# Hand-ordering an FFT-mixing and max-out-MLP kernel: an earlier first transform, a second buffer for its result, and a re-ordered startup

## The chip, the cores and the metric

The kernel runs on one core of one Trainium2 chip. The metric is device time in microseconds (us). Lower is better. The kernel before took 677.96 us (median of 15 runs). Runs of one kernel scatter: the kernel before stays within 674.8 to 683.2 us over 15 runs. So a single run says nothing about differences of a few us, and comparisons below use runs that were made on the same chip in turn. Experiments of different rounds are compared by their ratios to the kernel before, which ran in each round.

## The reference

For each of 8 batches, x (3072 x 256) is filtered along its length: real FFT, product with a filter, inverse FFT. The result goes through a two-branch max layer.

```python
X = np.fft.rfft(x, axis=1)                         # x: 8 x 3072 x 256
y = np.fft.irfft(X * (filt_r + 1j * filt_i), n=3072, axis=1)
x2 = y.reshape(8 * 3072, 256)
out = np.maximum(x2 @ w1, x2 @ w2) @ w_out         # w1, w2: 256 x 1024; w_out: 1024 x 256
```

## The kernel before

The length is split as 3072 = 128 x 24, so that the transforms become matmuls in four steps. Each batch passes through them like this:

- **f1** (12 pieces): `pa = C1 * x`, evicted (copied out of PSUM) by ScalarE (ACT) to `at`, written to DRAM as `ad`, and read back in another order as `bt`.
- **f2** (16 groups): `px = U * bt`; VectorE (DVE) multiplies by the filter `F` into `pqt`; `pz = VP * pqt + VQ * pqt` goes by way of `zt` to DRAM as `zd`, and is read back re-ordered as `zr`.
- **s4** (6 per batch): `py = zr * G1`, the last part of the inverse transform, giving `y` for one token tile.
- **moe** (6 tiles of 8 steps): `ph = Wd * y` with Wd = w1 - w2, a ReLU into `gt`, then `po = M * y + Wo * gt` with Wo = w_out and M = w2 * w_out, because max(a, b) = b + relu(a - b).

A batch of the main loop has 48 steps. In batch b the loop does moe for batch b, f2 for b+1 and f1 for b+2. A scheduler orders the instructions of each engine. PE is the matmul engine (TensorE). SP (SyncE) and POOL (GpSimd) mainly issue the DMA transfers here, each through its own queue, and POOL also makes tables.

```python
xpool = ...(name="xpool", bufs=2)     # x of one batch: 3 loads of 512 KB
apool = ...(name="apool", bufs=3)
bpool = ...(name="bpool", bufs=1)     # bt
...
def gen_f1(b):
    for c in range(12):
        ...                            # pa = C1 * x piece, at <- pa, every second c: ad <- at (SP)
        if c == 11:                    # then bt <- ad, 8 transfers on the SP queue
            ...
        yield
...
load_w(); load_x(1)
drain(gen_f1(0)); tables_pe(); prep_w()
...
drain(gen_f2(0)); drain(gen_f1(1)); s4(0)

for b in range(B + 1):
    ...
    for i in range(6):
        for j in range(8):
            moe_h(tt, j); moe_o(tt - 1, j)
            step = 8 * i + j
            if step % 2 == 0:
                next(f2, None)
            elif step >= 12:           # f1 of the batch after next starts here
                next(f1, None)
            if j == 4 and tt + 1 < 6 * B and i < 5:
                s4(tt + 1)
        if i == 5:
            drain(f2); drain(f1)
            s4(tt + 1)                 # first tile of the next batch, at the very end
```

## Time and profile before

| | before |
|---|---|
| span of the profiled run | 677.3 us |
| until the first px of the main loop | 134.3 us |
| from there to the end | 543.0 us |
| distance between first px of batches 0 and 1, 1 and 2 | 72.0, 72.4 us |

The first view is the page's row of 40 equal slices, here of 16.9 us each. A digit is the busy share in tenths. PEclk is the granted TensorE clock, and DMA is the mean busy share of the 16 DMA engines.

```profile
PE   0342293299987999699969996999989997999997
...
PEclk9856556589997999799979998899989998999999
DMA  9999528723495249623882369333842484234112
```

The left fifth is the startup: PE does little, and the DMA engines are at 9 in the first four slices. Later PE mostly reads 9, but falls to 6 or 7 again and again, and the clock falls with it. The chain of waits (what released what, followed back from the last instruction) sums to this, by engine:

```profile
PE 66%; DMA 22%; SPq 7%; ACT 2%; issue 1%; DVE 1%; DVEq 0%; ACTq 0%
```

22% of the span hangs on a DMA, though the matmuls are the work. The chain in order of time shows where. Its columns are the start in us, the length in us, and what. These are its longest pieces of the startup:

```profile
1.59 12.18 DMA w2f<-in_moe_w_dram
...
19.66 10.49 DMA ad<-at
...
50.94 9.19 SPq L273
60.17 9.87 SPq L273
...
74.41 5.78 DMA F<-zrow
...
108.32 11.04 DMA zr__600<-zd
119.44 4.29 DMA ad<-at
...
128.35 5.87 DMA bt__662<-ad
```

`SPq L273` is the SP queue issuing the `bt<-ad` transfers. Each of those two pieces takes over 9 us to issue. And these are successive pieces at the end of batch 1:

```profile
255.71 11.47 DMA zr__2076<-zd
267.25 4.10 DMA ad<-at
272.70 5.82 DMA bt__2125<-ad
278.65 0.63 PE px L298 x2
```

PE is not in this chain for about 23 us. For part of that it still has older work, but not to the end. The table of stretches shows this for the end of batch 0, where the chain leaves PE in the same way from 183.6 us on. Its columns are the stretch, its length, then busy us (and count) of PE, PE weight loads, DVE, ACT and POOL, the granted clock, the DMA share and GB/s:

```profile
200.00:206.50 6.50, 1.52 (x11) 0.87 (x9) 1.29 (x2) 0.00 (x0) 0.00 (x0) 0.87 0.86 190
206.50:214.00 7.50, 7.28 (x38) 4.75 (x39) 5.34 (x6) 3.35 (x6) 0.00 (x0) 0.66 0.42 80
```

PE works 1.5 of 6.5 us, and afterwards the granted clock averages 0.66 for 7.5 us. The start times of `px` by batch (minimum, median and maximum ns of one, then first and last start in us) give the period:

```profile
L298 PE MATMUL px<-bt__662,U x32: 270/274/417, 134.3 to 175.2; 96*96 96x256 bf16 x32
L298 PE MATMUL px<-bt__1305,U x32: 270/274/421, 206.3 to 247.2; 96*96 96x256 bf16 x32
L298 PE MATMUL px<-bt__2125,U x32: 270/274/421, 278.7 to 319.2; 96*96 96x256 bf16 x32
```

### The profile page before, as it was taken

The numbers are of one execution on the slowest core, as the hardware profiler recorded it, in microseconds if no ns is written. First come the engines' busy times: TensorE is split into PE (matmuls) and PEld (weight loads), VectorE is DVE, ScalarE is ACT, GpSimd is POOL, SyncE is SP. The second block draws the span as 40 slices with busy tenths as digits, with TensorE's granted clock in tenths as the row PEclk, the third lists the DMA queues.
The fourth block names the chain that finished last, engine by engine and source line by source line (L and its number), as shares of the span: only waits on it lengthen the run. The fifth ranks groups of instructions, "written<-read, shape, count | busy, mean of one in ns | idle before, by whom it ended". The sixth has DMA issues, their size and how long they took to land.

```text
span 677.3 us, 9992 instructions
## 1 busy us (share of the span) xinstructions
PE 548.2 (81%) x3939; PEld 402.7 (59%) x4008; DVE 362.0 (53%) x465; ACT 302.2 (45%) x537; POOL 30.3 (4%) x60
## 2 busy tenths in 40 slices
PE   0342293299987999699969996999989997999997
PEld 0131281177765777477647774677667775777775
DVE  2520280087636764477438742776377646864543
ACT  2450043156624663256416651566246634554441
POOL 5330000000000000000000000000000000000000
PEclk9856556589997999799979998899989998999999
DMA  9999528723495249623882369333842484234112
GB/s 233 135 135 193 112 70 193 184 54 143 128 252 120 99 144 227 172 86 112 206 210 101 126 160 235 89 115 139 199 110 98 145 203 116 68 129 124 63 63 93
DMA packets 82144, 94.51 MB, mean 140 GB/s; under 512 B 6737, under 2 KB 59986, under 8 KB 82002
## 3 DMA queue, kind: packets, MB, share of 16 engines
q1 hardware_dynamic: 73058, 77.62, 40.0%
q0 software_dynamic: 9040, 16.26, 16.8%
q8 instruction: 31, 0.51, 0.3%
q14 instruction: 15, 0.12, 0.1%
HBM read 59.77 MB, written 50.33 MB: 163 GB/s over the span
## 4 chain that ended last, share of the span: by engine, by line
PE 66%; DMA 22%; SPq 7%; ACT 2%; issue 1%; DVE 1%; DVEq 0%; ACTq 0%
PE ph L340 21%; PE po L365 19%; DMA ad<-at 6%; SPq L273 5%; PE px L298 5%; PE pz L288 5%; PE po L360 5%; PE pz L289 5%; PE py L324 3%; PE pa L264 2%; DMA w2f<-in_moe_w_dram 2%; DMA zr__2896<-zd 2%; DMA zr__1256<-zd 2%; DMA zr__2076<-zd 2%; DMA zr__600<-zd 2%
## 5 line engine op out<-in xcount | busy, mean ns | idle before, releaser
L365 PE MATMUL po<-Wo,gt 128*128 128x256 bf16 x1536 | 231.2, 273 | 1.1
L345 ACT ACTIVATE gt<-ph 128x512 bf16<-128x512 f32 x240 | 141.5, 593 | 161.2 <-PE ph L340 158.5
L301 DVE TENSOR_TENSOR pqt<-px,F 96x1024 bf16<-96x1024 f32 x128 | 155.5, 1218 | 96.6 <-PE px L298 75.5
L365 PEld LDWEIGHTS <-gt 128*128 128x128 bf16 x1536 | 149.8, 98 | 58.6 <-issue 1.4
L290 ACT ACTIVATE zt<-pz 96x512 bf16<-96x512 f32 x128 | 75.9, 593 | 132.3 <-PE pz L289 120.8
L343 DVE TENSOR_SCALAR gt<-ph 128x512 bf16<-128x512 f32 x144 | 99.0, 687 | 59.1 <-PE ph L340 55.3
L367 DVE COPY ot<-po 128x512 f32<-128x512 f32 x96 | 66.0, 691 | 89.4 <-PE po L365 69.2
L340 PEld LDWEIGHTS <-Wd 128*128 128x128 bf16 x768 | 76.0, 101 | 25.5 <-issue 6.6
L288 PE MATMUL pz<-pqt,VP 96*96 96x256 bf16 x256 | 70.7, 298 | 5.8 <-DVE pqt L301 5.6
L289 PE MATMUL pz<-pqt,VQ 96*96 96x256 bf16 x256 | 71.1, 300 | 0.0
L298 PEld LDWEIGHTS <-U 96*96 96x96 bf16 x256 | 34.3, 141 | 59.5 <-issue 42.0
L265 ACT ACTIVATE at<-pa 128x512 bf16<-128x512 f32 x96 | 55.5, 598 | 28.5 <-PE pa L264 13.3
L289 PEld LDWEIGHTS <-VQ 96*96 96x96 bf16 x256 | 34.7, 135 | 8.7 <-issue 7.4
L288 PEld LDWEIGHTS <-VP 96*96 96x96 bf16 x256 | 35.1, 137 | 1.4 <-DVE pqt L301 0.7
L264 PEld LDWEIGHTS <-C 128*128 128x128 bf16 x96 | 10.3, 108 | 23.8 <-ACT C L114 17.9
L298 PE MATMUL px<-bt__269,U 96*96 96x256 bf16 x32 | 9.9, 418 | 13.8 <-DMA bt__269<-ad 13.8
L264 PE MATMUL pa<-t__91,C 128*128 128x512 bf16 x12 | 5.3, 632 | 17.9 <-ACT C L114 17.9
L298 PE MATMUL px<-bt__662,U 96*96 96x256 bf16 x32 | 6.8, 298 | 12.5 <-DMA bt__662<-ad 12.5
L222 DVE CAST VQ<-pw 96x480 bf16<-96x480 f32 (+1 forms) x7 | 4.3, 611 | 17.9 <-PE pw L221 17.9
L324 PE MATMUL py<-G,zr__600 128*128 128x128 bf16 x48 | 4.1, 234 | 10.7 <-DMA zr__600<-zd 10.7
L217 PEld LDWEIGHTS <-U 96*96 96x96 bf16 x32 | 3.8, 187 | 12.1 <-ACT U L173 6.2
L298 PE MATMUL px<-bt__3765,U 96*96 96x256 bf16 x32 | 6.9, 300 | 4.1 <-DMA bt__3765<-ad 4.1
(347 smaller groups left out, 591.4 us busy)
## 6 DMA issues: line engine op xcount, KB each, us to landing
out_dram<-ot SPq DMA_DIRECT2D x48, 512.0 KB
ad<-at SPq DMA_DIRECT2D x48, 256.0 KB
zd<-zt SPq DMA_DIRECT2D x64, 192.0 KB
t__91<-in_x_dram POOLq DMA_DIRECT2D x3, 512.0 KB, 12.0
bt__269<-ad SPq DMA_DIRECT2D x8, 192.0 KB
t__216<-in_x_dram POOLq DMA_DIRECT2D x3, 512.0 KB, 16.7
t__684<-in_x_dram POOLq DMA_DIRECT2D x3, 512.0 KB, 18.3
zr__600<-zd SPq DMA_DIRECT2D x12, 128.0 KB
```

Source lines behind the costliest of these rows:

```text
L265: S.activation(at[:, 2 * (c % 2):2 * (c % 2) + 2], pa, AF.Copy)
L273: nc.sync.dma_start(out=bt_[24 * rs:24 * rs + 24, 16 * h:16 * h + 16], in_=src)
L288: TE.matmul(pz[:, i], VP[:, 2 * g + i], pqt[:, 0, i], start=True, stop=False)
L289: TE.matmul(pz[:, i], VQ[:, 2 * g + i], pqt[:, 1, i], start=False, stop=True)
L290: S.activation(zt[:, 2 * (g % 2):2 * (g % 2) + 2], pz, AF.Copy)
L298: TE.matmul(px[:, i], U[:, 2 * g + i].rearrange("p a b c -> p (a b c)"), bt_[:, 2 * g + i], start=True, stop=True)
L301: V.tensor_tensor(pqt, px.rearrange("p (o i) d -> p o i d", o=1).to_broadcast([QP, 2, 2, D]), F[:, :, 2 * g:2 * g + 2], OP.mult)
L340: TE.matmul(ph, Wd[:, dc, 128 * j:128 * j + 128], y_[:, dc].rearrange("p a b -> p (a b)"), start=(dc == 0), stop=(dc == 1))
L343: V.tensor_scalar(gt[tt][:, j], ph, 0.0, None, OP.max)
L345: S.activation(gt[tt][:, j], ph, AF.Relu)
L365: TE.matmul(p_, g_[:, jj, 128 * n:128 * n + 128], Wo[:, jj], start=False, stop=(jj == 7))
L367: V.tensor_copy(ot[tt][:, n - 1:n + 1], po[tt])
```

## The change

Its intent: have the transforms of later batches ready before the loop needs them, so that PE has no gap at batch ends, and shorten the startup. The diff, cut to its core:

```diff
-    xpool bufs=2, apool bufs=3, bpool bufs=1
+    xpool bufs=16 (12 pieces per batch), apool bufs=4, bpool bufs=2
+    ctx.enter_context(tc.manual_schedule())      # each engine runs in the order as written
...
+    # startup: x0 in 12 loads first, table C1, f1(0); then the other tables, F, weights, x1;
+    # row 0 of the filters in small fp32 loads on SP, and the groups with t=0 come last in f2
-        kk = init.tile([QP, T, 2, 2, J], FP32)   # 4 iotas, innermost run 12
+        kk = init.tile([QP, T, 2, J, 2], FP32)   # 2 iotas, innermost run 2
...
-        if j in (1, 4, 6):                       # ReLU on DVE, else on ACT
+        if j in (1, 5):
...
-            nc.sync.dma_start(out=dst..., in_=ot[tt])
+            (nc.sync if b == B - 1 else G).dma_start(out=dst..., in_=ot[tt])
...
-    load_w(); load_x(1); drain(gen_f1(0)); tables_pe(); prep_w(); ...
-    drain(gen_f2(0)); drain(gen_f1(1)); s4(0)
+    load_f0(); table_c(); drain(gen_f1(0)); tables_u()
+    load_f(1, 16); load_f(16, 32); load_w(); (load_x(1, c) for 12 c); tables_pe()
+    f2 = gen_f2(0); 17 x next(f2); prep_w(); ...
+    drain(f2); drain(gen_f1(1))
+    G.dma_start(out=gate, in_=bt[1][95:96, 31, 0:16])   # x2's loads wait here for bt(1)
+    (load_x(2, c) for 12 c); s4(0)
...
-                elif step >= 12:
-                    next(f1, None)
-                if j == 4 and tt + 1 < 6 * B and i < 5:
-                    s4(tt + 1)
-            if i == 5: drain(f2); drain(f1); s4(tt + 1)
+                else:
+                    if b > 0 or step >= 5:
+                        next(f1, None)
+                    if b + 3 < B and step < 24:
+                        load_x(b + 3, step // 2)
+                if j == (4 if i < 5 else 6) and tt + 1 < 6 * B:
+                    s4(tt + 1)
```

More of the change, by code (lines that the diff above doesn't have):

```diff
@@ L57 @@
     G1 = const.tile([128, 128], BF16)
-    U = const.tile([QP, T, 2, 2, 24], BF16)
+    U = const.tile([QP, T, 2, 48], BF16)
     VP = const.tile([QP, T, QP], BF16)
@@ L67 @@
     dram = ctx.enter_context(tc.tile_pool(name="dram", bufs=2, space=bass.MemoryType.DRAM))
-    xpool = ctx.enter_context(tc.tile_pool(name="xpool", bufs=2))
-    apool = ctx.enter_context(tc.tile_pool(name="apool", bufs=3))
-    bpool = ctx.enter_context(tc.tile_pool(name="bpool", bufs=1))
+    xpool = ctx.enter_context(tc.tile_pool(name="xpool", bufs=16))
+    apool = ctx.enter_context(tc.tile_pool(name="apool", bufs=4))
+    bpool = ctx.enter_context(tc.tile_pool(name="bpool", bufs=2))
     pqpool = ctx.enter_context(tc.tile_pool(name="pqpool", bufs=4))
@@ L74 @@
     pso = ctx.enter_context(tc.tile_pool(name="pso", bufs=2, space=bass.MemoryType.PSUM))
-    xb = {}
-    def load_x(b):
-        t_ = xpool.tile([128, N2, D], BF16, tag="xb")
-        src = x[b].rearrange("(p n) d -> p n d", n=N2)
-        for c in range(3):
-            G.dma_start(out=t_[:, 8 * c:8 * c + 8, :], in_=src[:, 8 * c:8 * c + 8, :])
-        xb[b] = t_
-    load_x(0)
+    zrpool = ctx.enter_context(tc.tile_pool(name="zrpool", bufs=2))
     setup = ExitStack()
     init = setup.enter_context(tc.tile_pool(name="init", bufs=1))
-    if True:
+    ctx.enter_context(tc.manual_schedule())
@@ new lines, with load_x, fsrc, load_f @@
+    xb = {}
+    def load_x(b, c):
+        t_ = xpool.tile([128, 2, D], BF16, tag="xb", name="xb")
+        src = x[b].rearrange("(p n) d -> p n d", n=N2)
+        G.dma_start(out=t_, in_=src[:, 2 * c:2 * c + 2, :])
+        xb[b, c] = t_
+    def fsrc(f, row0, dm, nm, dt, nt):
+        return bass.AP(f.tensor, f.offset + row0 * D, [[dm * D, nm], [dt * D, nt], [1, D]])
+    def load_f(t0, t1):
+        for ri, f in enumerate((filt_r, filt_i)):
+            for dr in range(2):
+                row0, dt = (t0, 1) if dr == 0 else (64 - t0, -1)
+                for q in range(2):
+                    p0 = 48 * q + 24 * dr
+                    G.dma_start(out=F[p0:p0 + 24, ri, t0:t1], in_=fsrc(f, row0, 64, 24, dt, t1 - t0))
@@ new lines, with load_f0 @@
+    F0 = init.tile([QP, 2, D], FP32)
+    def load_f0():
+        for ri, f in enumerate((filt_r, filt_i)):
+            for dr in range(2):
+                for mm, row0 in enumerate((0, 96) if dr == 0 else (32, 64)):
+                    for q in range(2):
+                        p0 = 48 * q + 24 * dr + mm
+                        if p0 == 48:
+                            nc.sync.dma_start(out=F0[48:49, ri], in_=f[1536:1537, :])
+                            nc.sync.dma_start(out=F0[50:72:2, ri], in_=fsrc(f, 128, 128, J - 1, 1, 1))
+                        else:
+                            nc.sync.dma_start(out=F0[p0:p0 + 23:2, ri], in_=fsrc(f, row0, 128, J, 1, 1))
@@ new lines @@
+    SW = init.tile([QP, QP], BF16)
+    zero = init.tile([128, 1], FP32)
+    pid = init.tile([128, 1], FP32)
+    G.iota(pid, pattern=[[1, 1]], base=0, channel_multiplier=1,
+           allow_small_or_imprecise_dtypes=True)
+    kc = init.tile([128, 2, 2, T], FP32)
+    G.iota(kc[:, :, 0], pattern=[[0, 2], [1, T]], base=0, channel_multiplier=0,
+           allow_small_or_imprecise_dtypes=True)
+    G.iota(kc[:, :, 1], pattern=[[0, 2], [-1, T]], base=64, channel_multiplier=0,
+           allow_small_or_imprecise_dtypes=True)
@@ new lines, with table_c @@
+    for c in range(12):
+        load_x(0, c)
+    def table_c():
+        V.memset(kc[:, :, 1, 0:1], 32.0)
+        V.memset(kc[:, 1, 0, 0:1], 64.0)
+        V.memset(zero, 0.0)
+        p128 = init.tile([128, 1], FP32)
+        V.tensor_scalar(p128, pid, 1.0 / 128.0, None, OP.mult)
+        uc = init.tile([128, 2, 2, T], FP32)
+        rc = init.tile([128, 2, 2, T], FP32)
+        V.tensor_scalar(uc[:, 0], kc[:, 0], p128, 0.25, OP.mult, OP.add)
+        V.tensor_scalar(uc[:, 1], kc[:, 1], p128, 0.5, OP.mult, OP.add)
+        V.tensor_scalar(uc[:, 1, 0, 0:1], kc[:, 1, 0, 0:1], p128, 0.25, OP.mult, OP.add)
+        V.tensor_scalar(rc, uc, RND, RND, OP.add, OP.subtract)
+        V.tensor_tensor(uc, uc, rc, OP.subtract)
+        S.activation(C1, uc.rearrange("p a b c -> p (a b c)"), AF.Sin, bias=zero, scale=TWO_PI)
@@ L92, with tables_u @@
+    def tables_u():
         V.memset(I128, 0.0)
@@ L94 @@
                         fill=1.0, base=0, channel_multiplier=1)
-        zero = init.tile([128, 1], FP32)
-        V.memset(zero, 0.0)
-        pid = init.tile([128, 1], FP32)
-        G.iota(pid, pattern=[[1, 1]], base=0, channel_multiplier=1,
-               allow_small_or_imprecise_dtypes=True)
-        kc = init.tile([128, 128], FP32)
-        G.iota(kc[:, 0:65], pattern=[[1, 65]], base=0, channel_multiplier=0,
-               allow_small_or_imprecise_dtypes=True)
-        G.iota(kc[:, 65:128], pattern=[[1, 63]], base=1, channel_multiplier=0,
-               allow_small_or_imprecise_dtypes=True)
-        p128 = init.tile([128, 1], FP32)
-        V.tensor_scalar(p128, pid, 1.0 / 128.0, None, OP.mult)
-        uc = init.tile([128, 128], FP32)
-        rc = init.tile([128, 128], FP32)
-        V.tensor_scalar(uc[:, 0:65], kc[:, 0:65], p128, 0.25, OP.mult, OP.add)
-        V.tensor_scalar(uc[:, 65:128], kc[:, 65:128], p128, 0.5, OP.mult, OP.add)
-        V.tensor_scalar(rc, uc, RND, RND, OP.add, OP.subtract)
-        V.tensor_tensor(uc, uc, rc, OP.subtract)
-        S.activation(C1, uc, AF.Sin, bias=zero, scale=TWO_PI)
+        V.memset(SW, 0.0)
+        G.affine_select(out=SW, in_=SW, pattern=[[-1, QP]], compare_op=OP.not_equal,
+                        fill=1.0, base=-48, channel_multiplier=1)
+        G.affine_select(out=SW, in_=SW, pattern=[[-1, QP]], compare_op=OP.not_equal,
+                        fill=-1.0, base=48, channel_multiplier=1)
+        kk = init.tile([QP, T, 2, J, 2], FP32)
+        G.iota(kk[:, :, 0], pattern=[[1, T], [128, J], [64, 2]], base=0,
+               channel_multiplier=0, allow_small_or_imprecise_dtypes=True)
+        G.iota(kk[:, :, 1], pattern=[[-1, T], [128, J], [64, 2]], base=64,
+               channel_multiplier=0, allow_small_or_imprecise_dtypes=True)
+        G.iota(kk[:, 0, 0], pattern=[[128, J], [96, 2]], base=0,
+               channel_multiplier=0, allow_small_or_imprecise_dtypes=True)
+        G.iota(kk[:, 0, 1], pattern=[[128, J], [32, 2]], base=32,
+               channel_multiplier=0, allow_small_or_imprecise_dtypes=True)
         pq = pid[0:QP]
@@ L138 @@
         V.tensor_tensor(mk[:, 2:3], mk[:, 0:1], mk[:, 3:4], OP.subtract)
-        kk = init.tile([QP, T, 2, 2, J], FP32)
-        for s_ in range(2):
-            G.iota(kk[:, :, s_, 0, :], pattern=[[1, T], [128, J]], base=32 * s_,
-                   channel_multiplier=0, allow_small_or_imprecise_dtypes=True)
-            G.iota(kk[:, :, s_, 1, :], pattern=[[-1, T], [128, J]], base=128 - 32 * s_,
-                   channel_multiplier=0, allow_small_or_imprecise_dtypes=True)
-        uu = init.tile([QP, 2, T, 2, 2, J], FP32)
@@ L147 @@
-        ru = init.tile([QP, 2, T, 2, 2, J], FP32)
-        for q in range(2):
-            for h in range(2):
-                V.tensor_scalar(uu[:, q, :, :, h, :], kk[:, :, :, h, :], n2s, off[:, q, h:h + 1],
-                                OP.mult, OP.add)
-            V.tensor_scalar(ru[:, q], uu[:, q], RND, RND, OP.add, OP.subtract)
-            V.tensor_tensor(uu[:, q], uu[:, q], ru[:, q], OP.subtract)
-            for s_ in range(2):
-                S.activation(U[:, :, q, s_, :],
-                             uu[:, q, :, s_].rearrange("p t h j -> p t (h j)"),
-                             AF.Sin, bias=zero[0:QP], scale=mk[:, s_:s_ + 1])
@@ L160 @@
-        k0 = init.tile([QP, 2, 2, J], FP32)
-        u0 = init.tile([QP, 2, 2, J], FP32)
-        r0 = init.tile([QP, 2, 2, J], FP32)
-        G.iota(k0, pattern=[[0, 2], [64, 2], [128, J]], base=0, channel_multiplier=0,
-               allow_small_or_imprecise_dtypes=True)
-        V.memset(k0[:, 1, 0, 0:1], 1536.0)
-        V.tensor_scalar(u0[:, 0], k0[:, 0], n2s, 0.25, OP.mult, OP.add)
-        V.tensor_scalar(u0[:, 1], k0[:, 1], n2s, 0.5, OP.mult, OP.add)
-        V.tensor_scalar(u0[:, 1, 0, 0:1], k0[:, 1, 0, 0:1], n2s, 0.25, OP.mult, OP.add)
@@ L169 @@
-        V.tensor_scalar(r0, u0, RND, RND, OP.add, OP.subtract)
-        V.tensor_tensor(u0, u0, r0, OP.subtract)
-        for q in range(2):
-            for h in range(2):
-                S.activation(U[:, 0, q, 0, J * h:J * h + J], u0[:, q, h, :], AF.Sin,
-                             bias=zero[0:QP], scale=mk[:, 2 + h:3 + h])
-        SW = init.tile([QP, QP], BF16)
-        V.memset(SW, 0.0)
-        G.affine_select(out=SW, in_=SW, pattern=[[-1, QP]], compare_op=OP.not_equal,
-                        fill=1.0, base=-48, channel_multiplier=1)
@@ L181 @@
-        G.affine_select(out=SW, in_=SW, pattern=[[-1, QP]], compare_op=OP.not_equal,
-                        fill=-1.0, base=48, channel_multiplier=1)
-        def fsrc(f, row0, dj, dt, nt):
-            return bass.AP(f.tensor, f.offset + row0 * D, [[dj * D, J], [dt * D, nt], [1, D]])
-        zrow = init.tile([1, D], BF16)
-        V.memset(zrow, 0.0)
-        nyq = init.tile([1, D], FP32)
-        nyb = init.tile([1, D], BF16)
-        for ri, f in enumerate((filt_r, filt_i)):
-            for q in range(2):
-                for s_ in range(2):
-                    p0 = 48 * q + 24 * s_
-                    G.dma_start(out=F[p0:p0 + J, ri], in_=fsrc(f, 32 * s_, 128, 1, T))
-                    t0 = 1 if s_ == 0 else 0
-                    G.dma_start(out=F[p0 + J:p0 + 24, ri, t0:T],
-                                in_=fsrc(f, 128 - 32 * s_ - t0, 128, -1, T - t0))
-                G.dma_start(out=F[48 * q + J:48 * q + 24, ri, 0:1], in_=fsrc(f, 64, 128, 1, 1))
@@ L201 @@
-        nc.sync.dma_start(out=nyq, in_=filt_r[1536:1537, :])
-        V.tensor_scalar(nyb, nyq, 0.5, None, OP.mult)
-        nc.sync.dma_start(out=F[48:49, 0, 0], in_=nyb)
-        nc.sync.dma_start(out=F[48:49, 1, 0], in_=zrow)
-        V.tensor_scalar(F[0:1, 0, 0], F[0:1, 0, 0], 0.5, None, OP.mult)
-        V.memset(F[0:1, 1, 0], 0.0)
+        uu = init.tile([QP, 2, T, 2, J, 2], FP32)
+        ru = init.tile([QP, T, 2, J, 2], FP32)
+        for q in range(2):
+            for mm in range(2):
+                V.tensor_scalar(uu[:, q, :, :, :, mm].rearrange("p t r j -> p t (r j)"),
+                                kk[:, :, :, :, mm].rearrange("p t r j -> p t (r j)"),
+                                n2s, off[:, q, mm:mm + 1], OP.mult, OP.add)
@@ new lines, in tables_u @@
+        for q in range(2):
+            V.tensor_scalar(uu[:, q, 0, 0, :, 0], kk[:, 0, 0, :, 0], n2s, 0.25 + 0.25 * q, OP.mult, OP.add)
+            V.tensor_scalar(uu[:, q, 0, 1, :, 1], kk[:, 0, 1, :, 1], n2s, 0.25 + 0.25 * q, OP.mult, OP.add)
+        V.tensor_scalar(uu[:, 1, 0, 0, 0, 0:1], pn, 0.5, 0.25, OP.mult, OP.add)
+        for q in range(2):
+            V.tensor_scalar(ru, uu[:, q], RND, RND, OP.add, OP.subtract)
+            V.tensor_tensor(uu[:, q], uu[:, q], ru, OP.subtract)
+        Uv = U.rearrange("p t q (r j m) -> p t q r j m", r=2, m=2)
@@ new lines, in tables_u @@
+        for q in range(2):
+            for dr in range(2):
+                for mm in range(2):
+                    s_ = (mm + dr) % 2
+                    S.activation(Uv[:, :, q, dr, :, mm], uu[:, q, :, dr, :, mm],
+                                 AF.Sin, bias=zero[0:QP], scale=mk[:, s_:s_ + 1])
+            S.activation(Uv[:, 0, q, 0, :, 0], uu[:, q, 0, 0, :, 0], AF.Sin,
+                         bias=zero[0:QP], scale=mk[:, 2:3])
+            S.activation(Uv[:, 0, q, 1, :, 1], uu[:, q, 0, 1, :, 1], AF.Sin,
+                         bias=zero[0:QP], scale=mk[:, 3:4])
@@ L209, in tables_pe @@
+        e0 = init.tile([QP, 2], FP32)
+        V.tensor_scalar(e0[:, 0:1], pm, 0.0, None, OP.is_equal)
+        V.tensor_scalar(e0[:, 1:2], e0[:, 0:1], -1.0, 1.0, OP.mult, OP.add)
+        V.tensor_scalar(e0[:, 0:1], e0[:, 0:1], -0.5, 1.0, OP.mult, OP.add)
+        for ri in range(2):
+            V.tensor_scalar(F[:, ri, 0], F0[:, ri], e0[:, ri:ri + 1], None, OP.mult)
     def tables_pe():
@@ L216, in tables_pe @@
             for i in range(n):
-                TE.matmul(pv[:, i], U[:, t + i].rearrange("p a b c -> p (a b c)"),
+                TE.matmul(pv[:, i], U[:, t + i].rearrange("p a b -> p (a b)"),
                           I128[0:QP, 0:QP], start=True, stop=True)
@@ L257, in gen_f1 @@
     def gen_f1(b):
-        xt = xb[b]
         ad = dram.tile([128, N2, D], BF16, tag="ad")
@@ L263, in gen_f1 @@
             pa = ps.tile([128, 2, D], FP32, tag="ps")
-            TE.matmul(pa, C1, xt[:, 2 * c:2 * c + 2], start=True, stop=True)
+            TE.matmul(pa, C1, xb[b, c], start=True, stop=True)
             S.activation(at[:, 2 * (c % 2):2 * (c % 2) + 2], pa, AF.Copy)
@@ L294, in gen_f2 @@
         zt = None
-        for g in range(16):
+        for g in list(range(2, 16)) + [0, 1]:
             px = ps.tile([QP, 2, D], FP32, tag="ps")
             for i in range(2):
-                TE.matmul(px[:, i], U[:, 2 * g + i].rearrange("p a b c -> p (a b c)"),
+                TE.matmul(px[:, i], U[:, 2 * g + i].rearrange("p a b -> p (a b)"),
                           bt_[:, 2 * g + i], start=True, stop=True)
@@ L307, in gen_f2 @@
         s3(*pend.pop(0))
+        if b == 0:
+            yield
         zr_ = zrpool.tile([128, N2, D], BF16, tag="zr")
@@ L370, in moe_o @@
             dst = out[b * N:(b + 1) * N].rearrange("(p n) d -> p n d", n=N2)
-            nc.sync.dma_start(out=dst[:, 4 * i:4 * i + 4], in_=ot[tt])
+            (nc.sync if b == B - 1 else G).dma_start(out=dst[:, 4 * i:4 * i + 4], in_=ot[tt])
     def drain(g):
@@ L376, in drain @@
             pass
+    load_f0()
+    table_c()
+    drain(gen_f1(0))
+    tables_u()
+    load_f(1, 16)
+    load_f(16, 32)
     load_w()
-    load_x(1)
-    drain(gen_f1(0))
+    for c in range(12):
+        load_x(1, c)
     tables_pe()
+    f2 = gen_f2(0)
+    for _ in range(17):
+        next(f2)
     prep_w()
     setup.close()
-    zrpool = ctx.enter_context(tc.tile_pool(name="zrpool", bufs=2))
     ypool = ctx.enter_context(tc.tile_pool(name="ypool", bufs=3))
@@ L387 @@
     opool = ctx.enter_context(tc.tile_pool(name="opool", bufs=2))
-    drain(gen_f2(0))
+    drain(f2)
     drain(gen_f1(1))
+    gate = const.tile([1, 16], BF16)
+    G.dma_start(out=gate, in_=bt[1][95:96, 31, 0:16])
+    for c in range(12):
+        load_x(2, c)
     s4(0)
-    def nothing():
-        return
-        yield
     for b in range(B + 1):
-        f2 = gen_f2(b + 1) if b + 1 < B else nothing()
-        if b + 2 < B:
-            load_x(b + 2)
-            f1 = gen_f1(b + 2)
-        else:
-            f1 = nothing()
+        f2 = gen_f2(b + 1) if b + 1 < B else iter(())
+        f1 = gen_f1(b + 2) if b + 2 < B else iter(())
         for i in range(6):
@@ L405 @@
             for j in range(8):
+                step = 8 * i + j
                 if tt < 6 * B:
@@ L409 @@
                     moe_o(tt - 1, j)
-                step = 8 * i + j
                 if step % 2 == 0:
                     next(f2, None)
-                elif step >= 12:
-                    next(f1, None)
-                if j == 4 and tt + 1 < 6 * B and i < 5:
-                    s4(tt + 1)
-            if i == 5:
-                drain(f2)
-                drain(f1)
-                if tt + 1 < 6 * B:
+                else:
+                    if b > 0 or step >= 5:
[3 more added lines that the diff above has]
+                if j == (4 if i < 5 else 6) and tt + 1 < 6 * B:
                     s4(tt + 1)
```

## The prediction

> **What bounds the kernel now.** The chain of waits shows three stretches. (1) A startup of 134 us, until the first px of the main loop (134.25 us). Its chain: the weights' load w2f<-in (12.2 us, its consumers being first on ACT and DVE), ad<-at writes (10.5 and 7.8 us), the bt<-ad issues at L273 held up on the SP queue (about 24 us), the tiny F<-zrow (5.8 us), f2(0) at half clock (about 22 us), then zr<-zd 11.0, ad<-at 4.3, bt<-ad 5.9 us. PE is busy 3.5 of 26 us in 108–134. (2) A loop of 539 us. Inside a batch PE is dense (9.9 of 10 us, granted clock 1.00). At each batch end the chain leaves PE: zr<-zd 11.7, ad<-at 4.0, bt<-ad 5.4 us. In 200–206.5 PE is busy 1.5 us, then about 4 us run at clock 0.50. Period 72.5 us with x loads, about 69 without. (3) A tail of 4.4 us.
>
> **What the change does.** Order is by hand. Startup: x0 first in 12 pieces, the tables and first transform before filters and weights; row-0 filters come separately by SP, and use of t=0 is moved last. Loop: bt has two buffers, x 16 small ones, so f1(b+2) runs in odd steps from step 1 instead of 13, bt lands while f2 still runs, and zr (issued after step 32) has 14 steps before its user; output stores move from SP to POOL; one ReLU in eight moves from DVE (687 ns) to ACT (593 ns).
>
> **Cost, loop.** Loop columns: 8·(49152+61440+6144) for ph, po, py, 7·24576 for px, pz and 6·6144 for pa, = 1,142,784. The trace's dense half-clock matmuls take 0.213 us per 256 columns, full-clock ones 0.107, so 476 us at full clock. Dense pairs of steps take 2.83 us where columns give 2.77, i.e. 2.2% more: about 487 us. Add one warm-up (2–3 us) and about 3 us of small stalls: 493 us. Per 8 steps with f1 and f2 ACT needs about 8.9 us, DVE 8.3, PE 11.7, so PE stays the limit. Gain about 46 us, all critical. The clock falls when PE idles and recovers under load, as the Trainium skill says (TensorE: Matmul & The Clock Gate, Part 1: The HAM clock gate); the trace agrees (0.50, then 1.00 from 140 us).
>
> **Cost, startup (estimate from the trace's durations).** x0 and first transform to 15 us; kk on POOL after the 12 x issues, uu on DVE, U by about 26; VP/VQ 11 us: 37; f2(0) 22: 59; prep_w 9; f1(1) 8; ad landing 2–3; half of bt 5: first px at about 86 us. x2's loads are gated behind bt(1), so they no longer take DMA from zr, ad and bt. Gain about 48 us.
>
> Sum: 86 + 493 + 4.4 = 583 us; range 567 to 602. Faster by over 2%: 0.98; within 2%: 0.015; slower: 0.005.
>
> **What would show it.** First px of the loop at 78–95 us (was 134). Slices: no dip of PE at batch ends, PEclk 1.0 from then on; period 62.5–64.5 us for batches with f1 and f2. Chain: PE above 80%, zr, ad and bt gone after startup.
>
> **What would make it wrong.** F's small-row loads delaying the first pqt (startup near 100 us); zr or y arriving late at step 46; head-of-line waits in ACT or DVE under the fixed order and rotating PSUM buffers (period 66 us or more); POOL-issued stores slow to free ot; a lower granted clock under unbroken PE load.

## The result, and the profile after

The changed kernel took 601.67 us (median of 12 runs, 596.58 to 608.6). Ratios here are the mean time of one kernel's fast runs over that of the other's fast runs of the same rounds, so they are not quite the ratio of the medians quoted. The ratio is 0.8867, with a 95% interval of 0.8834 to 0.8901: faster by 11.3%. The predicted time was 583 us with a range of 567 to 602, so the result sits at the upper edge of the range, 0.3 us inside it.

A run that is over 1.5% above the fastest of its kernel is called slow here and left out of the ratios. The first profiled run was one (608.6 us, though its granted clock of 0.981 is within that of the others, 0.979 to 0.988). The kernel was therefore run once more without an edit, and everything shown of "after" is from that run.

> The changed kernel once more, unedited, to have a profile in the fast state. If the waits seen at the ends of batches 1 and 2 in the first profile (2.0 and 1.6 us, with a clock dip of a few us behind the first) are chance of the DMA load, they will be of another size or in another batch here and the span will be shorter by as much; the first px of the loop should stay within 2 us of 102.7, because that delay has causes fixed in the program. Clean batches should again be 62.7 us apart.

It took 603.27 us (4 runs; ratio 0.8912, interval 0.8875 to 0.895). The profiled run, of 599.7 us span, was fast. The waits at the ends of batches 1 and 2 did change (1.3 us where 2.0 had been, for one), and clean batches are 62.7 us apart. But the first px came at 98.2 us and not within 2 us of 102.7: the startup itself varies. VectorE waited 11.7 us for the filter F in the first profile and 7.6 us in this one. Five profiles of kernels with this very startup (this one, the first, and three experiments below) have it at 97.7, 98.0, 98.2, 99.5 and 102.7 us.

| | before | after |
|---|---|---|
| until the first px of the loop | 134.3 | 98.2 |
| from there to the end | 543.0 | 501.5 |
| span | 677.3 | 599.7 |

The slices (15.0 us each), and the chain's shares by engine, of the changed kernel:

```profile
PE   4055864899999999999999999999999999999996
...
PEclk9999985799999999999999999999999999999999
DMA  7999786985977777578965987688336832261112
```

```profile
PE 79%; DMA 13%; POOL 3%; SPq 1%; ACT 1%; issue 1%; DVE 1%; DVEq 0%; POOLq 0%
```

From the ninth slice to the last but one PE stays at 9, and the clock to the end: the dips at batch ends are gone. What is left at the left edge is shorter, but PE still reads between 0 and 8 there, and DMA between 6 and 9. The longest pieces of the chain in that stretch are now these:

```profile
9.25 4.80 POOL kk L160
14.05 4.78 POOL kk L162
...
24.59 12.88 DMA F<-in_filt_i_dram
37.76 20.70 DMA F<-in_filt_i_dram
...
84.11 3.79 DMA ad<-at
...
95.39 8.02 DMA bt__717<-ad
```

The weights' load, the long `bt` issues of the SP queue (pieces of at most 1.4 us are left) and the tiny `F<-zrow` are gone from it. Two of the filter loads `F`, 13 and 21 us from issue to landing, have taken their place. The second was issued when the first had landed, and PE idled 6.5 us behind it. The start times of px by batch:

```profile
L318 PE MATMUL px<-bt__717,U x32: 270/274/421, 98.2 to 146.2; 96*96 96x256 bf16 x32
L318 PE MATMUL px<-bt__1270,U x32: 270/272/275, 166.2 to 209.5; 96*96 96x256 bf16 x32
L318 PE MATMUL px<-bt__2044,U x32: 270/272/275, 230.5 to 273.8; 96*96 96x256 bf16 x32
L318 PE MATMUL px<-bt__2884,U x32: 270/272/275, 293.6 to 336.9; 96*96 96x256 bf16 x32
```

The second gap is 64.3 us (it ends with a wait of 1.3 us for `zr`), the third 63.1, and the later ones, not shown, are 62.7 to 62.8 us. The old loop had 72.0 to 72.7 us in its first four gaps and 69.4 and 69.3 in its last two. The first gap now is 68.0 us. One line of PE's timeline tells why: the number in brackets is the idle time before the instruction, in us, and what ended it.

```profile
107.82 0.61 PE L284 MATMUL pa<-xb,C 128*128 128x512 bf16 x1 [2.51 <-DMA xb<-in_x_dram]
```

PE takes its instructions in the written order, so it stood still for 2.5 us (3.9 in the first profile) until a piece of x2 had landed. Those loads had been gated behind `bt(1)`. After the pause the matmuls run at half rate again: the `pa` above takes 0.61 us and a normal one 0.38.

### The profile page after: what moved, and what is told of

Its sections match the earlier page's. It is cut to its first block, busy times and chain, and to the rows that moved or that the text cites. A ratio compares the mean times of both kernels' runs of the same rounds, so it can differ in the third digit from the quotient of the medians.

```text
span 606.8 us, 10173 instructions
## 1 busy us (share of the span) xinstructions
PE 534.0 (88%) x3939; PEld 396.1 (65%) x4008; DVE 332.7 (55%) x420; ACT 331.3 (55%) x588; POOL 98.0 (16%) x170
## 4 chain that ended last, share of the span: by engine, by line
PE 78%; DMA 14%; POOL 3%; issue 2%; ACT 1%; SPq 1%; DVE 1%; DVEq 0%; POOLq 0%
PE po L387 27%; PE ph L362 23%; PE po L382 7%; DMA F<-in_filt_i_dram 6%; PE pz L308 5%; PE pz L309 5%; PE px L318 5%; PE py L346 3%; PE pa L284 3%; DMA zd<-zt 2%; DMA xb<-in_x_dram 1%; DMA bt__717<-ad 1%; DMA zr__2214<-zd 1%; POOL F L101 1%; POOL kk L160 1%
## 5 line engine op out<-in xcount | busy, mean ns | idle before, releaser
L367 ACT ACTIVATE gt<-ph 128x512 bf16<-128x512 f32 x288 | 170.7, 593 | 109.1 <-PE ph L362 104.2
L362 PEld LDWEIGHTS <-Wd 128*128 128x128 bf16 x768 | 74.0, 99 | 18.8 <-issue 3.3
L393 POOL DMA_DIRECT2D out_dram<-ot x42 | 22.6, 537 | 384.2 <-DVE ot L389 375.8
L365 DVE TENSOR_SCALAR gt<-ph 128x512 bf16<-128x512 f32 x96 | 65.4, 682 | 24.5 <-PE ph L362 24.5
L309 PE MATMUL pz<-pqt,VQ 96*96 96x256 bf16 x256 | 69.0, 293 | 0.0
L88 POOL DMA_DIRECT2D xb<-in_x_dram x96 | 51.3, 551 | 25.4 <-DMA F<-in_filt_r_dram 9.3
L284 PE MATMUL pa<-xb,C 128*128 128x512 bf16 x96 | 38.1, 409 | 11.6 <-DMA xb<-in_x_dram 10.9
L318 PEld LDWEIGHTS <-U 96*96 96x96 bf16 x256 | 32.7, 135 | 12.9 <-issue 11.0
L238 PE MATMUL pv<-I,U 96*96 96x96 bf16 x32 | 4.0, 283 | 17.7 <-ACT U L218 17.7
L318 PE MATMUL px<-bt__717,U 96*96 96x256 bf16 x32 | 6.9, 300 | 8.4 <-DMA bt__717<-ad 8.4
L197 DVE TENSOR_SCALAR uu<-kk,n2s,off 96x768 f32<-96x768 f32 x4 | 2.5, 684 | 15.3 <-POOL kk L166 15.3
```

What stands on the lines that cost most here:

```text
L284: TE.matmul(pa, C1, xb[b, c], start=True, stop=True)
L309: TE.matmul(pz[:, i], VQ[:, 2 * g + i], pqt[:, 1, i], start=False, stop=True)
L318: TE.matmul(px[:, i], U[:, 2 * g + i].rearrange("p a b -> p (a b)"), bt_[:, 2 * g + i], start=True, stop=True)
L362: TE.matmul(ph, Wd[:, dc, 128 * j:128 * j + 128], y_[:, dc].rearrange("p a b -> p (a b)"), start=(dc == 0), stop=(dc == 1))
L365: V.tensor_scalar(gt[tt][:, j], ph, 0.0, None, OP.max)
L367: S.activation(gt[tt][:, j], ph, AF.Relu)
```

## The experiments

Two groups of questions: what in the loop closed the gaps, and why the startup was shorter by 36 us and not 48.

### The loop: the early f1, or the second buffer?

**late_f1** puts the start of f1 back and keeps two buffers:

```diff
-                    if b > 0 or step >= 5:
+                    if step >= 12:
                         next(f1, None)
```

> Changed kernel with f1 starting at step 13 of a batch again, two bt buffers kept. Theory A (the early start of f1 removes the gap, because bt can only be read back after ad is written and SP takes zr first): bt lands about 20 us after step 35, the user is 13 us away, so about 7 us of wait and 2 us of clock loss in each of batches 0 to 5: 640 to 660 us. Theory B (the second bt buffer removes the gap): within 8 us of the changed kernel.

Measured: 646.83 us (4 runs), ratio 0.9561 (0.9505 to 0.9618). So 44 us of the gain are lost, as theory A says and theory B does not. The list of waits (us in total, times, longest) has one such line for each of six batches, 5.3 to 7.4 us:

```profile
PE px L318 <- DMA bt__2246<-ad: 7.4, 1, 7.4
```

The SP queue shows the mechanism. This is its timeline in late_f1 near the end of batch 1 (start, us taken to issue, what):

```profile
218.17 5.74 SPq L334 DMA_DIRECT2D zr__2197<-zd  x12
224.01 0.40 SPq L287 DMA_DIRECT2D ad<-at  x1
230.12 6.81 SPq L293 DMA_DIRECT2D bt__2246<-ad  x8
```

And this is the same batch of the changed kernel:

```profile
200.95 0.34 SPq L287 DMA_DIRECT2D ad<-at  x1
203.11 6.97 SPq L293 DMA_DIRECT2D bt__2044<-ad  x8
...
220.47 7.80 SPq L334 DMA_DIRECT2D zr__2214<-zd  x12
```

With the late start, the last `ad` write queues behind the twelve `zr` reads (218 to 224 us). Then `bt` has to wait until that write has landed, and it is issued at 230 us, 8.7 us before its user ran at 238.8. With the early start `bt` is issued at 203 us, 27 us before its user, and `zr` has the queue to itself afterwards.

**one_bt** keeps the early f1 and takes the second buffer away (`bpool` with `bufs=1`).

> Changed kernel with one bt buffer, f1 early. Theory A: bt must wait for the last px at step 30 and holds SP up to then, so three zd writes and zr come late, and s4 at step 46 waits 2 to 5 us in six batches: plus 10 to 25 us. Theory B: the whole loop gain is lost, plus 40 us or more. If buffers do not matter at all: within 4 us.

Measured: 613.43 us (4 runs), ratio 0.9065 (0.9025 to 0.9104), about 10 us slower than the unedited kernel in the same rounds. SP's timeline of the same batch:

```profile
209.95 6.12 SPq L293 DMA_DIRECT2D bt__2044<-ad  x8
...
224.50 5.78 SPq L334 DMA_DIRECT2D zr__2214<-zd  x12
```

`bt` now waits for the last px of the old contents (issued at 210 and not at 203 us), and `zr` behind it goes at 224.5 in place of 220.5. The next batch's first `py` then waits 1.7 to 2.9 us for `zr` in each of six batches. Theory A's account and size hold, at the low end of its range.

**late_one** undoes both, so it is nearly the old loop behind the new startup. The written order, the stores on POOL, the split of the ReLUs, the small x pieces and s4 at step 46 stay as in the changed kernel.

> Changed kernel with both undone: one bt buffer and f1 from step 13. Theory A: the same as late_f1 alone within 6 us. Theory B: clearly slower than late_f1, by 30 us or more. Either way near 650 us, for the old loop lost about 9.8 us in each of the first batches against a clean 62.7 us; this kernel has the new startup, so it also tells how much of the gain is the startup's: about 30 us if the old gaps return whole.

Measured: 649.56 us (4 runs), ratio 0.9601 (0.9556 to 0.9646). That is within 3 us of late_f1 alone: with a late f1 the second buffer is worth next to nothing. All that lies outside these two edits is worth 4.0%, 27 us. That is not the startup alone: the first px comes 36.6 us sooner than before (97.7 us), but from there to the end late_one takes 549.9 us where the kernel before took 543.0. Its last two gaps are 72.4 and 73.3 us and were 69.4 and 69.3. Which part of the change costs these 7 us behind a late f1 was not tested.

**loop_only** asks the opposite: the kernel before, with its own order by the scheduler, its startup, its x loads, its stores on SP and three of eight ReLUs on DVE, and only this edit:

```diff
-    bpool bufs=1
+    bpool bufs=2
...
-                elif step >= 12:
+                else:
                     next(f1, None)
-                if j == 4 and tt + 1 < 6 * B and i < 5:
-                    s4(tt + 1)
-            if i == 5: drain(f2); drain(f1); s4(tt + 1)
+                if j == (4 if i < 5 else 6) and tt + 1 < 6 * B:
+                    s4(tt + 1)
```

> The kernel before (its order, startup, x loads, SP stores, three ReLUs of eight on DVE) with only the loop's part: two bt buffers, f1 from step 1 of each batch, s4 of the next batch at step 46. Theory A (the early f1 is the loop's gain): batches 62.7 to 65 us apart, as in the changed kernel, startup still about 134 us: 625 to 640 us. Rival (the hand-written order and the stores on POOL are needed too): batches 67 us or more apart, above 650 us.

Measured: 633.11 us (4 runs), ratio 0.934 (0.9305 to 0.9375). The start times of px by batch:

```profile
L298 PE MATMUL px<-bt__662,U x32: 269/274/417, 132.8 to 173.5; 96*96 96x256 bf16 x32
L298 PE MATMUL px<-bt__1105,U x32: 270/272/276, 195.2 to 237.0; 96*96 96x256 bf16 x32
L298 PE MATMUL px<-bt__1925,U x32: 270/272/276, 259.1 to 301.0; 96*96 96x256 bf16 x32
```

The startup is the old one (132.8 us), and the batches are 62.4 to 65.3 us apart. So the loop's gain needs neither the hand-written order, nor stores on POOL, nor the smaller x pieces, nor the other split of the ReLUs. The edit still holds three things. late_f1 and one_bt separate the early f1 from the second buffer. s4's move to step 46 is in late_f1 too, so it is not enough by itself, but no run takes it away from an early f1. From the first px to the end loop_only takes 498.0 us, less than the changed kernel's 501.5, for its x2 is there in time (no matmul of f1 waits for x in its loop). The two halves nearly add up: 6.6% for the loop alone and 4.0% for the rest alone (late_one), 10.9% for both in the same rounds as the latter.

### The startup: a chain of work, or the DMA engines?

Theory C: POOL's slow tables, and the late issue of F behind them, set the startup. Theory D: from 20 to 70 us the DMA engines carry all they can, so that moving one transfer only moves the wait.

**iota** gives the table kk another layout, so that the innermost run of each iota is 12 elements and not 2:

```diff
-        kk = init.tile([QP, T, 2, J, 2], FP32)
-        G.iota(kk[:, :, 0], pattern=[[1, T], [128, J], [64, 2]], base=0, ...)      # and one more
+        kk = init.tile([QP, 2, T, 2, J], FP32)
+        for mm in range(2):
+            for r, sg in ((0, 1), (1, -1)):
+                G.iota(kk[:, mm, :, r], pattern=[[sg, T], [128, J]], base=64 * r + 64 * mm, ...)
```

> Changed kernel with kk laid out so that the innermost run of its iotas is 12 long and not 2. The two iotas of 4.8 us should cost about 0.65 us per 384 elements again, so POOL is free about 7 us sooner. Theory C (POOL's late tables and late issue of F set the startup): U and F come 5 to 7 us sooner, first px of the loop 92 to 94 us, 595 to 598 us. Theory D (the DMA engines' throughput sets when F is there): U comes sooner but the wait of pqt for F grows by as much, first px moves 2 us or less.

The edit worked as such. The old form is in the chain above (4.80 and 4.78 us for 768 elements per partition each). The first line below is the new form (min, median and max ns, 384 elements each), the second is px of the first batch:

```profile
L162 POOL IOTA kk<- x4: 588/600/939, 9.0 to 10.9; 96x384 f32 x4
```

```profile
L317 PE MATMUL px<-bt__215,U x32: 417/420/422, 46.5 to 72.8; 96*96 96x256 bf16 x32
```

POOL saves about 7 us, and the filter loads are issued 7 us sooner. But the first f2 starts at 46.5 us, later than the 42.4 of the unedited kernel: PE has its tables by 40 us and then waits 6.7 us for `bt(0)`, whose transfers SP starts to issue at 28.3 and not 20.7 us. That the earlier F loads delay them is an inference from the overlap in time. Measured: 602.83 us (4 runs), ratio 0.889 (0.8859 to 0.8921), which is no change. Theory C falls. Theory D's outcome holds, though not its way: it expected a longer wait of pqt for F, and the wait for `bt(0)` came in its place. My own prediction had missed these iotas (it costed them as before), yet that miss did not set the time.

**fcopy** loads only half of F from DRAM (both halves of the partitions hold the same rows) and makes the other half by two transfers within SBUF:

```diff
-                for q in range(2):
-                    p0 = 48 * q + 24 * dr
-                    G.dma_start(out=F[p0:p0 + 24, ri, t0:t1], in_=...)
+                p0 = 24 * dr
+                G.dma_start(out=F[p0:p0 + 24, ri, t0:t1], in_=...)
...
+        G.dma_start(out=F[48:96, :, t0:t1], in_=F[0:48, :, t0:t1])    # after the loads, twice
```

> Changed kernel with the second copy of F (partitions 48 to 95) made from the first by two transfers within SBUF in place of eight of the sixteen loads from DRAM. Theory D (the F loads' many small rows among other traffic set f2(0)): the wait of pqt for F (6.5 and 11.7 us in two profiles) falls below 3 us and the first px of the loop comes 5 to 10 us sooner: 592 to 597 us. Theory C: within 2 us of the changed kernel.

Measured: 595.34 us (4 runs), ratio 0.8777 (0.8745 to 0.8809). The time is about what theory D expected, but its profile does not show the expected way. The longest wait of a pz for pqt is 5.0 us (6.5 in the unedited kernel), the chain instead waits 11.9 us for `zd` writes inside f2(0), and the first px still comes at 98.2 us. The profiled run was the slowest of the four (598.28), so it may not be typical. What it wins lies behind the first px: from there to the end it takes 498.3 us, and the unedited kernel 501.5. How the median came down is left open.

**w_small** takes traffic away without touching anything else. Of w1 and w2 only 64 of 1024 columns are loaded, and the rest is set to constants.

```diff
-        nc.sync.dma_start(out=w1f, in_=...)          # and w2f
+        nc.sync.dma_start(out=w1f[:, :, 0:64], in_=...[:, :, 0:64])
...
+        V.memset(w1f[:, :, 64:HID], 0.02)            # at the start of tables_u; w2f 0.01
```

> Changed kernel, wrong on purpose: of w1 and w2 only 64 of 1024 columns are loaded and the rest is set to constants by two DVE memsets while DVE is idle, so about 1.97 MB leave the DMA queues between 34 and 70 us; the kernel's other work is the same. Theory D (the startup's middle, 20 to 70 us, is bound by the DMA engines): the waits inside f2(0) for F and for zd shrink and the first px of the loop comes 5 to 8 us sooner than 98 to 102. Rival (the startup is a chain of latencies and of POOL's work): within 2 us.

The result is wrong. Measured: 594.96 us (4 runs), ratio 0.8767 (0.8739 to 0.8794). The first px comes at 91.5 us, 6.2 us sooner than the earliest of the five profiles of this startup. (They are from another chip. combo_a and combo_b, on w_small's chip, have it at 98.1 and 98.3 us.) The last F load is issued at almost the same time as in the unedited kernel, but takes 12.9 us to land and not 20.7:

```profile
38.76 12.86 DMA F<-in_filt_i_dram
```

The same stretch in the unedited kernel and in w_small, with columns as in the table of stretches above:

```profile
40.00:60.00 20.00, 10.84 (x49) 8.23 (x48) 9.94 (x10) 4.44 (x8) 3.75 (x7) 1.00 1.18 241
```

```profile
40.00:60.00 20.00, 17.31 (x80) 13.96 (x79) 15.95 (x15) 6.81 (x12) 6.76 (x12) 1.00 1.19 197
```

The DMA engines are as full as before (1.18 and 1.19). But PE does 17.3 us of work in it and not 10.8, because F is there sooner: PE's waits behind it come to 1.8 us in all, and were 7.9. The SP queue's weights thus delay POOL's filter loads. The Trainium skill (DMA: Bandwidth & Descriptors, section "Issuing engines are not separate DMA queues") says that transfers started by different engines end up on the same 16 DMA engines and interleave there, and this fits that: 1.97 MB less on SP's queue, and POOL's last F load lands 7.8 us sooner after its issue. Theory D stands for this stretch.

### The gate, and versions that combine

**x_ahead** loads four pieces of x2, for which there are free buffers, ahead of the gate:

```diff
     for c in range(12):
         load_x(1, c)
+    for c in range(4):
+        load_x(2, c)
...
     G.dma_start(out=gate, in_=bt[1][95:96, 31, 0:16])
-    for c in range(12):
+    for c in range(4, 12):
         load_x(2, c)
```

> Changed kernel with four of the twelve pieces of x2 loaded ahead of the gate, into the four free buffers. If the gate is what makes the first pa of the loop wait (3.9 and 4.4 us in two profiles), that wait goes, and with it a clock dip of about 2 us behind it: 597 to 599 us, first period about 63 to 64.5 us in place of 66.9 to 68. If those four loads collide with zr, ad and bt of the startup, the first px of the loop comes later by as much and nothing is won.

Measured: 595.3 us (4 runs), ratio 0.8787 (0.8758 to 0.8816). The px of its first two batches:

```profile
L318 PE MATMUL px<-bt__725,U x32: 269/274/421, 99.5 to 141.0; 96*96 96x256 bf16 x32
L318 PE MATMUL px<-bt__1270,U x32: 269/273/275, 160.8 to 204.1; 96*96 96x256 bf16 x32
```

The first period is 61.3 us and was 68.0, and the first px comes 1.3 us later (99.5), inside the scatter of the startup. From the first px to the end it takes 493.9 us. So the gate cost the changed kernel 6.7 us in the first batch.

**combo_a** is fcopy and x_ahead together:

> fcopy and x_ahead together. Ratio to before was 0.878 for each alone, 0.889 for the changed kernel. If their gains add: 0.868, about 588 us. If both only won the same wait of the first batch for x2: 0.877.

Measured: 594.74 us (4 runs), ratio 0.8767 (0.8736 to 0.8798). It was run on another chip. The two gains do not add. The ratio is the 0.877 that the expectation gave for the case that both only won the same wait for x2.

**combo_b** also moves the weights' products behind f1(1):

```diff
-    prep_w(); setup.close(); ...
-    drain(f2); drain(gen_f1(1))
+    drain(f2); drain(gen_f1(1))
+    prep_w(); setup.close(); ...
```

> combo_a, and prep_w moved behind f1(1), so that the weights' products are made on PE while ad and bt of the startup are under way. The chain after f2(0) loses prep_w's piece (w2b 1.9, pt 1.8, pm 2.8 to 3.4 us in the chain of waits): first px 5 to 7 us sooner than in combo_a, about 582 us. If the ad and bt transfers, and not the compute ahead of them, are what the first px waits for there, then 2 us or less.

Measured: 593.66 us (4 runs), ratio 0.8746 (0.8719 to 0.8773), with the first px at 98.3 us. The 6.5 us of prep_w left the chain, and the first px did not move. SP's timeline tells why. First the unedited kernel, then combo_b:

```profile
76.43 5.75 SPq L334 DMA_DIRECT2D zr__655<-zd  x12
...
91.19 5.56 SPq L293 DMA_DIRECT2D bt__717<-ad  x8
```

```profile
76.40 5.74 SPq L336 DMA_DIRECT2D zr__601<-zd  x12
...
91.06 5.54 SPq L295 DMA_DIRECT2D bt__663<-ad  x8
```

In both, SP issues the `zr` reads when the last `zd` write has landed, and the first `ad` write right behind them, at 82.3 us. In the unedited kernel prep_w and the first piece of f1(1) end at 82.1 us, the same time. So prep_w lay beside another path that was as long, and taking it away won nothing. This is the lesser case of the expectation.

**combo_c** is combo_b with the faster iota:

> combo_b and the faster iota. The iota alone won nothing (602.8 us), because F's earlier loads met bt(0), whose landing moved from 42 to 46 us. With half of F's loads from DRAM gone, theory D gives 0 to 3 us sooner; if the iota still gains nothing, DMA throughput is again the limit before f2(0).

Measured: 596.86 us (4 runs), ratio 0.8803 (0.877 to 0.8835), with the first px at 101.2 us. The iota gains nothing here either: all four runs are slower than combo_b's (596.76 to 598.29 against 592.47 to 593.9 us), by 3 us in the median.

combo_b has the lowest median of the correct kernels, 593.66 us, and its interval lies wholly below that of the changed kernel, by ratio to the same kernel before. It does not lie clear of fcopy's, x_ahead's or combo_a's.

## Why the prediction was right or wrong

- **Direction and most of the size: right.** Predicted 583 us, measured 601.67 and 603.27. The gain was put at 95 us and was 73 to 76. In the two profiles, whose spans differ by 77.6 us, 36.1 of the 48 us put at the startup came true and 41.5 of the 46 put at the loop. That 601.67 lies within the range is in part luck, for the repeat's 603.27 does not.
- **The loop's mechanism: right.** Gaps at the batch ends were named as the loss, and the early f1 as what closes them. late_f1, one_bt and loop_only show that it is the early f1 (with s4's move to step 46 untested by itself). The second bt buffer, which the prediction named beside it, is worth 10 us and only together with it. The clean period of 62.7 us came out inside the predicted 62.5 to 64.5.
- **The loop's stalls: the term "about 3 us of small stalls" was too small.** The loop and tail were put at 497.4 us (493 + 4.4) and took 501.5. The first batch alone lost 6.7 us to the wait for gated x2 and the half rate behind it (68.0 us against 61.3 with x_ahead). The prediction had listed the gate only as a gain.
- **The startup: the term "first px of the loop at about 86 us" failed.** It came at 98.2 us, outside the stated 78 to 95. Its listed pieces sum to 83.5 us. Against those, f2(0) began at 42.4 us and not 37. It took 31.9 us to its last zt and not 22, with a wait of 6.5 us behind F inside. prep_w took about 6.7 and not 9, and the rest, f1(1) with ad and bt, 17.2 and not 15.5. For f2(0) the cause is that the sum treated DMA transfers as latencies that do not meet. "F's small-row loads delaying the first pqt" was named as a risk, and a wait for F is what the chain shows. w_small shows that most of it comes from throughput shared with the weights: f2(0) then takes 25.0 us, and the first px comes at 91.5. The later begin of f2(0) stays in w_small (42.4 us). It is the tables' iotas, costed too low, that put U at 31.6 and not 26 us. But iota shows that without them the begin is set by `bt(0)`, so the time is not won that way. The path after f2(0) was wrong too: the sum has prep_w in it, and combo_b shows that SP's issue of `zr` ahead of `ad` ends as late as prep_w does.
- **"POOL-issued stores slow to free ot", "head-of-line waits in ACT or DVE", "a lower granted clock under unbroken PE load": did not happen.** DVE's `ot` waits for PE alone, clean batches are at 62.7 us, and the clock stays at 1.00 from the second batch on (0.91 in the first, with its wait for x2).
- **"zr or y arriving late at step 46": happened, but small.** `py` waits 0.4 and 1.3 us for `zr` at the ends of batches 0 and 1, so `zr` is not wholly gone from the chain after the startup.
- **"Chain: PE above 80%": just missed,** at 79%.
- **Left open:** which of the startup's edits, one by one, won its 36 us over the kernel before (they were tested only as a whole), what delays it by the some 6 us that remain without the weights' traffic, what s4's move does by itself, what the moved stores and ReLUs do within the hand-written order, and how fcopy wins its time.

## What to carry to other kernels

When a result returns through DRAM to be re-ordered, look at the order on the queue that issues the round trip, and start the producer so early that its write has landed before the next group of transfers takes that queue. Here 12 steps earlier were worth 44 us, and an extra buffer alone almost nothing. In a startup where the DMA engines are full, count the bytes that must land before the first dependent step and ask which can be left out or wait. Adding up latencies, or speeding up the compute in front, predicts too much, and a piece of work counts only if no other path beside it ends as late. A gate that keeps prefetches out of a busy stretch must let through what an in-order engine will ask for first.

## What the Trainium skill lacked or had wrong

- GPSIMD Engine Reference (section 4.1 names iota as a GPSIMD operation): no page gives a cost of iota by its pattern. Here 768 elements per partition with an innermost run of 2 took 4.82 to 4.84 us, and 384 with an innermost run of 12 took 0.59 to 0.67 us but for one of 0.94, so about four times as much per element.
- TensorE: Matmul & The Clock Gate (Part 1) says that the default state is half rate. The durations agree: px of 256 columns took 0.42 us in the first f2, against 0.27 later. But the profile's granted clock reads 1.00 from the start to 80 us in the changed kernel, so that row is not to be trusted before its first change. Nor did load bring the full rate soon: in the first f2 of the kernel before, PE was busy 19.2 of the 21 us from 80 to 101 us, the clock read 0.50 and px took 0.42 us all the while. The page warns of unreliable clock events but does not name the first case.
- DMA: Bandwidth & Descriptors: the section cited above calls the streams interleaved, and no page gives a measured delay of POOL's transfers by SP's. Here 1.97 MB of weights on SP made the last F load of POOL take 20.7 us and not 12.9, and moved the first px of the loop by at least 6.2 us.
